# First two batches' memory matrix loaded dense on SP's queue and padded by POOL, first loads reordered: attention with memory and a gated MLP on one Trainium2 core

## The chip, the cores and the metric

The kernel runs on one core of a Trainium2 chip. The metric is the device time of one execution in microseconds (us); a kernel's time is the median over its runs. Engines are named as in the profile: PE (TensorE), DVE (VectorE), ACT (ScalarE), POOL (GpSimd) and SP (SyncE, which here only issues DMAs).

## The reference

Causal attention, mixed with a retrieval from a memory matrix M, followed by RMS norm and a gated MLP. B, H, S, D = 4, 8, 576, 64; the MLP has 2304 tokens, width 512 and inner width 1536, and its three weights arrive as float64.

```python
def _attn_ref(q, k, v, M_prev, z_prev, beta):
    scores = scale * np.matmul(q, k.transpose(0, 1, 3, 2))
    scores = np.where(causal, -1000000000.0, scores)
    a = np.exp(scores - scores.max(-1, keepdims=True))
    a /= a.sum(-1, keepdims=True) + 1e-09
    local = np.matmul(a, v)
    q_p = np.where(q > 0, q, np.exp(q) - 1.0) + 1.0
    mem_ret = np.einsum('bhsd,bhde->bhse', q_p, M_prev)
    mem_norm = np.einsum('bhsd,bhd->bhs', q_p, z_prev)[..., None] + 1e-06
    g = 1.0 / (1.0 + np.exp(-beta))[None, :, None, None]
    return g * mem_ret / mem_norm + (1 - g) * local
def _moe_ref(x, w_gate, w_val, w_out, rms_g):
    xn = x / np.sqrt(np.mean(x * x, axis=-1, keepdims=True) + 1e-06) * rms_g
    g = xn @ w_gate
    return (g / (1.0 + np.exp(-g)) * (xn @ w_val)) @ w_out
```

## The kernel before, in words

The 2304 tokens are 18 blocks of 128 rows; a block holds all 8 heads, 512 numbers of k, of v and of q per row. Blocks 0 and 1 are the first rows of batches 0 and 1. They are computed in float32, ahead of all else, so that the first chunk (two blocks) of the MLP can begin early. Later blocks use pairs of float16 numbers and transposes by DMA.

**The head, blocks 0 and 1** (L1026 to L1037). For a block n, PE transposes k and q (`prep_qk32`, L363), ACT and DVE make phi(q) (`phi_calc`, L347 to L349), PE makes the scores (`scores32`, L416), DVE masks them and finds the row minimum (L421), ACT takes the exponential (L430). PE transposes phi(q) and multiplies it with M (`mem32`, L442). M's place for this, `Mz`, is padded: 65 numbers per head in a row, of which the first 64 are M's and number 64 is z, so that one matmul gives both mem_ret and mem_norm. Its two halves of 64 partitions are equal copies of M, because heads with even and odd number lie in different halves; of the eight matmuls of a block, four read one half and four the other. Then `pv32` (transposes of the exponentials and L453), `evac32` (L465 to L482), `x_norm` and `x_float` (L696, L699) give the block's x, and xT0 of both blocks is what the first projections read (`m_proj`, L850).

**The weights.** w_gate and w_val come as 24 pieces of 128 x 512 float64 (512 KB each; w0 to w7 are the first third, t = 0, and so on) into a ring of six places. Each piece is converted by one ACT cast (L766) and two DVE operations (L767, L768). When a piece is converted, its place is free and the piece six later is loaded (`load_w`, L736). w_out's 12 pieces follow in the same way (`load_wo`, L756).

**The first loads.** `setup_small` puts beta, rms_g and z (twice) on ACT's queue. `HORD` (L26) gives the order of the first big loads: q0, k0, M0, q1, k1, M1, w0 to w5, where "k" brings k and v of a block. q, k, v and w go on SP's queue. M of the batches 0 and 1 goes on ACT's queue (L218), straight into the padded place; M of the batches 2 and 3 comes later, on SP's queue. POOL puts z into the padding (L222). POOL also issues eight loads of 256 KB (`load_pre`, L746), of k and v of later blocks of batches 0 and 1, for the column sums that set the scales (`gram`, L145); six are issued at once, two when places are free.

**What sets the order.** An engine takes its instructions in program order, and a scheduler writes that order from priorities and its own estimate of times; it decides anew for a changed program, also far behind the change. The loads of SP's and ACT's queues take eight completion semaphores in turn, both queues from one set; a load that is given a semaphore in use waits, on the engine that issues it, until the load that had it before has landed. Loads on POOL's queue have a set of their own.

Of the kernel before, what the change touches and what calls it, by code (L numbers as in the profile page):

```python
# [9 lines left out]
F32 = mybir.dt.float32  # L10
F16 = mybir.dt.float16
# [11 lines left out]
XSCALE = 2.0 ** 11  # L23
NEG = -1.0e38
HP = 0
HORD = "q0 k0 M0 q1 k1 M1 w0 w1 w2 w3 w4 w5"  # L26
LAG = 3
LAG0 = 8
NA = 2
# [27 lines left out]
def attn_memory_moe_kernel(  # L57
# [12 lines left out]
    nc = tc.nc  # L70
    B, D, H = M_prev.shape[:3]
# [3 lines left out]
    P = 128  # L75
# [11 lines left out]
    sb = ctx.enter_context(tc.tile_pool(name="sb", bufs=2))  # L87
# [50 lines left out]
    def gram(acc, src, first, last):  # L138
# [12 lines left out]
        out=ident, in_=ident, compare_op=ALU.is_equal, fill=0.0,  # L151
# [47 lines left out]
    def load_kv(n):  # L199
        tag = "kvt" if is_tail[n] else "kv"  # L200
        stage[n] = sb.tile([P, 2, HD], F32, tag=tag, name=f"kv{n}", bufs=1 if is_tail[n] else 4)
        if n < 2:
            for j in range(2):
                nc.sync.dma_start(out=stage[n][:, j], in_=qkv[n, :, j, :])
        else:
            nc.sync.dma_start(out=stage[n], in_=qkv[n, :, :2, :])

    def load_M(b):
        if b < 2:
            t = sb.tile([P, H, VW], F16, tag="v16", name=f"Mz{b}", bufs=10)  # L210
            Mz[b] = t.bitcast(F32)
            qst[("M", b)] = Mz[b][:, :, :D]
        else:
            qst[("M", b)] = sb.tile([P, HD], F32, tag="q", name=f"M{b}").rearrange(
                "p (h e) -> p h e", h=H
            )
        for hf in range(2):
            (nc.scalar if b < 2 else nc.sync).dma_start(  # L218
                out=qst[("M", b)][hf * D : (hf + 1) * D], in_=M_prev[b]
            )  # L220
        if b < 2:
            nc.gpsimd.tensor_copy(Mz[b][:, :, D], zz[:, b * H : (b + 1) * H])  # L222

    def load_q(n):
# [3 lines left out]
    def square_acc(src, acc):  # L228
        junk = sb.tile([P, HD], BF16, tag="junk", name="junk", bufs=1)
        np_ = src.shape[0]  # L230
        if len(src.shape) == 3:
            dst = junk[:np_].rearrange("p (h e) -> p h e", e=src.shape[2])
        else:
            dst = junk[:np_, : src.shape[1]]
        nc.scalar.activation(dst, src, AF.Square, accum_out=acc)  # L235
# [31 lines left out]
    def stat_M(b):  # L267

        cb[b] = const.tile([P, 8 + 2 * H], F32, name=f"cb{b}")
        ssm = tiny.tile([P, 3], F32, tag="mx", name=f"ssm{b}", bufs=2)  # L270
        square_acc(qst[("M", b)], ssm[:, 0:1])
        pow2_scales(over_partitions(ssm[:, 0:1], 1), 1, cb[b][:, 2:3], cb[b][:, 5:6])
        prep_M(b)

# [22 lines left out]
            tcb[b // 2] = t  # L297

    def prep_M(b):
        src = qst.pop(("M", b))  # L300
        m = sb.tile([P, 2, H, D + 2], F16, tag="M16", name=f"M16_{b}")
        M16[b] = m
        hi_cast(m[:, 0, :, :D], src, cb[b][:, 2:3])
        lo_cast(m[:, 1, :, :D], src, cb[b][:, 2:3], m[:, 0, :, :D])
        nc.gpsimd.tensor_copy(m[:, :, :, D], zhl[:, :, b * H : (b + 1) * H])
# [611 lines left out]


    def setup_small():
        nc.scalar.dma_start(out=beta_sb, in_=beta.rearrange("(o h) -> o h", o=1).to_broadcast([P, H]))  # L920
        nc.scalar.dma_start(out=rg, in_=rms_g)
        for r in range(2):
            nc.scalar.dma_start(out=zz[r * D : (r + 1) * D], in_=z_prev)

    gmax2 = const.tile([P, 1], F32, name="gmax2")

# [93 lines left out]
    pcs = [(m, cc, t) for t in range(NT3) for m in range(2) for cc in range(NC)]  # L1020
    setup_small()
    with tc.high_priority(HP) if HP else contextlib.nullcontext():
        for x in HORD.split():
            {"q": load_q, "k": load_kv, "M": load_M, "w": lambda p: load_w(*pcs[p])}[x[0]](int(x[1]))
    setup_consts()
    with tc.high_priority(PRIO[0]):  # L1026
        for n in range(2):
# [247 lines left out]
```

## Time and profile before

| what | value |
|---|---|
| timed runs | 654.41, 654.85, 657.68 us; median 654.85 us |
| the profiled execution | 659.15 us, of which the recorded span is 657.5 us |
| PE busy | 598.7 us (91% of the span) |
| DVE busy | 469.1 us (71%) |
| ACT busy | 384.5 us (58%) |
| POOL busy | 168.3 us (26%) |
| DMA, mean over the span | 135 GB/s |
| granted TensorE clock, mean over the span | 0.977 of full speed |

How to read it: the profile is one execution, and its times are counted from the start of the span. Busy time is that of instructions; a wait is put down to what ended it. The shares are averages over a span with very different stretches, so a question about the head is answered by views of the head: the lists of waits for a window, the timeline, and the table by stretches, which gives for each stretch the busy time and number of instructions of every engine, the granted clock (PEclk, 1.00 is 2.4 GHz and 0.50 is 1.2 GHz), the mean busy share of the 16 DMA engines and the GB/s that they moved.

### The profile page before, as it was taken

To read this page: it belongs to the slowest core of one execution; us is meant where nothing else is said; L and a number is where in the kernel's file an instruction comes from. 1 tells how busy PE (TensorE), PEld (TensorE's weight loads), DVE (VectorE), ACT (ScalarE), POOL (GpSimd) and SP (SyncE) were. 2 spreads that over 40 slices of the span, in tenths; PEclk is the share of its full clock that TensorE was granted. 3 is DMA by queue.
4 is the path that set the end of the run, shared out by engine and by line. 5 is a ranking of instruction groups with operands and counts; after the bars stand their busy time and mean duration, and the time that the engine had idled before them with its cause. 6 is when DMAs were issued, how large, how long until landed. Compare 5 with 4: busy or idle time off the path is not lost.

```text
span 657.5 us, 15991 instructions
## 1 busy us (share of the span) xinstructions
PE 598.7 (91%) x6120; PEld 467.7 (71%) x6120; DVE 469.1 (71%) x1444; ACT 384.5 (58%) x803; POOL 168.3 (26%) x251
## 2 busy tenths in 40 slices
PE   4569988997989679998999999899999999999996
PEld 3457876646757467786878677778777778878774
DVE  5489998878998656796876857968777667872221
ACT  4355667577688757575666656856666544442322
POOL 3020131122382323231242311522332212212211
PEclk9598998999999989999999999999999999999999
DMA  8897699639248798346848773495676573440001
GB/s 265 299 336 285 170 307 234 109 60 234 57 84 162 161 174 160 75 87 128 166 101 162 145 122 73 83 175 104 123 122 117 87 97 86 78 82 17 33 1 33
DMA packets 190636, 88.63 MB, mean 135 GB/s; under 512 B 175968, under 2 KB 175968, under 8 KB 190560
## 3 DMA queue, kind: packets, MB, share of 16 engines
q1 hardware_dynamic: 187360, 84.96, 60.3%
q0 software_dynamic: 640, 2.10, 0.9%
q8 instruction: 48, 0.79, 0.5%
q10 hardware_dynamic: 2560, 0.55, 0.5%
q14 instruction: 28, 0.23, 0.1%
HBM read 36.20 MB, written 4.72 MB: 62 GB/s over the span
## 4 chain that ended last, share of the span: by engine, by line
PE 50%; DMA 18%; DVE 17%; ACT 8%; issue 4%; SPq 1%; POOL 1%; ACTq 0%; DVEq 0%
PE gv L857 24%; DMA PT<-P 6%; PE out L912 4%; PE out L913 4%; PE out L914 4%; DMA kv<-in_qkv_dram 3%; DMA Mz<-in_M_prev_dram 2%; PE sc L500 2%; DVE P L566 2%; DMA xT<-x 2%; PE sc L526 2%; ACT junk L235 2%; DVE S L506 2%; DMA wo<-in_moe_w_out_dram 2%; DMA kT<-row 1%
## 5 line engine op out<-in xcount | busy, mean ns | idle before, releaser
L857 PE MATMUL gv<-xT,wgv 128*128 128x256 f16 x2304 | 314.1, 274 | 4.9 <-DVE th L871 2.9
L857 PEld LDWEIGHTS <-wgv 128*128 128x128 f16 x2304 | 220.9, 98 | 40.8 <-issue 6.7
L883 POOL TENSOR_TENSOR h<-th,h 128x256 f16<-128x256 f32 x96 | 72.0, 750 | 266.8 <-ACT h L882 214.4
L552 ACT ACTIVATE S<-S,nm 128x256 f32<-128x256 f32 (+4 forms) x128 | 75.4, 611 | 50.5 <-DVE nm L513 36.4
L500 PE MATMUL sc<-kT,qT 128*128 128x128 f16 x608 | 84.6, 220 | 2.0 <-DVE nm L506 1.4
L566 DVE TENSOR_TENSOR P<-S,P 128x512 f16<-128x512 f32 (+2 forms) x84 | 63.1, 751 | 31.5 <-ACT P L557 31.1
L868 DVE SCALAR_TENSOR_TENSOR th<-th,gv 128x256 f32<-128x256 f32 x96 | 39.8, 415 | 60.6 <-ACT th L867 60.2
L867 ACT ACTIVATE th<-gv,wt 128x256 f32<-128x256 f32 x96 | 45.0, 468 | 49.9 <-PE gv L857 49.7
L913 PE MATMUL out<-wo,h 128*128 128x512 f16 x192 | 73.1, 381 | 0.0
L912 PE MATMUL out<-wo,h 128*128 128x512 f16 x192 | 72.6, 382 | 0.2 <-ACT h L882 0.2
L914 PE MATMUL out<-wo,h 128*128 128x512 f16 x192 | 71.9, 380 | 0.0
L506 DVE CUSTOM_DVE_ANT_0 S<-sc,mask,qsc 128x256 f32<-128x256 f32 (+3 forms) x112 | 62.0, 574 | 10.0 <-PE sc L500 7.9
L557 ACT CAST P<-S 128x512 f16<-128x512 f32 (+2 forms) x100 | 59.7, 597 | 13.9 <-DMA PT<-P 12.4
L882 ACT CAST h<-th 128x256 f16<-128x256 f32 x96 | 38.6, 402 | 45.1 <-DVE th L871 44.5
L590 PE MATMUL loc<-v,PT 128*128 128x65 f16 x304 | 49.8, 194 | 16.3 <-DMA PT<-P 15.7
L500 PEld LDWEIGHTS <-qT 128*128 128x128 f16 x608 | 50.6, 98 | 7.2 <-issue 1.6
L592 PE MATMUL loc<-v,PT 128*128 128x65 f16 x304 | 49.5, 194 | 0.0
L591 PE MATMUL loc<-v,PT 128*128 128x64 f16 x304 | 49.5, 194 | 0.0
L850 PE MATMUL gv<-xT,wgv 128*128 128x256 f32 x192 | 46.1, 392 | 2.2 <-DVE h32e L871 1.8
L871 DVE SCALAR_TENSOR_TENSOR th<-th,wt,gv 128x256 f32<-128x256 f32 x96 | 45.7, 477 | 1.7
L590 PEld LDWEIGHTS <-PT 128*128 128x128 f16 x304 | 29.3, 98 | 23.1 <-DMA PT<-P 19.2
L850 PEld LDWEIGHTS gv<-xT,wgv 128*128 128x128 f32 x192 | 36.2, 195 | 8.1 <-DVE h32e L871 2.0
(222 smaller groups left out, 1096.6 us busy)
## 6 DMA issues: line engine op xcount, KB each, us to landing
kv<-in_qkv_dram SPq DMA_DIRECT2D x16, 512.0 KB, 4.8
wo<-in_moe_w_gate_dram SPq DMA_DIRECT2D x12, 512.0 KB, 7.4
wo<-in_moe_w_val_dram SPq DMA_DIRECT2D x12, 512.0 KB, 4.9
q<-in_qkv_dram SPq DMA_DIRECT2D x18, 256.0 KB, 3.5
wo<-in_moe_w_out_dram SPq DMA_DIRECT2D x8, 512.0 KB, 5.3
qT<-qT SPq DMA_DIRECT2D x32, 128.0 KB, 2.5
out_dram<-res SPq DMA_DIRECT2D x16, 256.0 KB, 2.3
pre<-in_qkv_dram POOLq DMA_DIRECT2D x8, 256.0 KB, 8.5
```

Of the source, the lines that this page charges most:

```text
L500: nc.tensor.matmul(t[:, g * w + j * P : g * w + (j + 1) * P], qT[n][:, t2, h, :], kT[blk_of[(b, j)]][:, h, :], start=(t2 == 0), stop=(t2 = ...
L506: nc.vector.tensor_tensor_reduce(out=s[:, g * w : (g + 1) * w], in0=t[:, g * w : (g + 1) * w], in1=mask[:, m0 : m0 + w], scale=qsc[n][:, 5:6],
L552: nc.scalar.activation(v_, v_, AF.Exp, bias=nm[:, g : g + 1], scale=-1.0)
L557: nc.scalar.copy(p16[:, : G * w], s[:, : G * w])
L566: eng.tensor_tensor(p16[:, w : 2 * w], s[:, :w], p16[:, :w], ALU.subtract)
L590: nc.tensor.matmul(a, phi_, vhi, start=(j == 0), stop=False)
L850: nc.tensor.matmul(o, wgv[:, 1 + p, o0 : o0 + P], xT[0][:, cc, :], start=(cc == 0), stop=(cc == NC - 1))
L857: nc.tensor.matmul(o, lhs, xT[c][:, rhs, :], start=(cnt == 0), stop=(cnt == 3 * NC - 1))
L883: nc.gpsimd.tensor_tensor(h16[:, 1], th, h16[:, 0], ALU.subtract)
L912: nc.tensor.matmul(o, hh, whi, start=(f == 0), stop=False)
L913: nc.tensor.matmul(o, hh, wlo, start=False, stop=False)
L914: nc.tensor.matmul(o, hl, whi, start=False, stop=(f == NF - 1))
```

## The change

M of the batches 0 and 1 is loaded on SP's queue into a dense tile (128 x 512, from the slots of `row16`, which the later blocks' splits use), and POOL copies it into the padded place; ACT's sum of squares of M reads the dense tile. k and v of the blocks 0 and 1 become loads of their own, and `HORD` is now k0, q0, M0, k1, q1, v0, M1, v1, w0 to w5. z, beta and rms_g are loaded on POOL's queue, z first.

```diff
-HORD = "q0 k0 M0 q1 k1 M1 w0 w1 w2 w3 w4 w5"
+HORD = "k0 q0 M0 k1 q1 v0 M1 v1 w0 w1 w2 w3 w4 w5"
...
-        if n < 2:
-            for j in range(2):
-                nc.sync.dma_start(out=stage[n][:, j], in_=qkv[n, :, j, :])
-        else:
+        if n >= 2:
             nc.sync.dma_start(out=stage[n], in_=qkv[n, :, :2, :])
+
+    def load_half(n, j):
+        nc.sync.dma_start(out=stage[n][:, j], in_=qkv[n, :, j, :])
...
             t = sb.tile([P, H, VW], F16, tag="v16", name=f"Mz{b}", bufs=10)
             Mz[b] = t.bitcast(F32)
-            qst[("M", b)] = Mz[b][:, :, :D]
+            t = sb.tile([P, H, 2, D], F16, tag="row16", name=f"M{b}")
+            qst[("M", b)] = t.rearrange("p h t e -> p (h t e)").bitcast(F32).rearrange(
+                "p (h e) -> p h e", h=H
+            )
...
         for hf in range(2):
-            (nc.scalar if b < 2 else nc.sync).dma_start(
-                out=qst[("M", b)][hf * D : (hf + 1) * D], in_=M_prev[b]
-            )
+            nc.sync.dma_start(out=qst[("M", b)][hf * D : (hf + 1) * D], in_=M_prev[b])
         if b < 2:
+            nc.gpsimd.tensor_copy(Mz[b][:, :, :D], qst[("M", b)])
             nc.gpsimd.tensor_copy(Mz[b][:, :, D], zz[:, b * H : (b + 1) * H])
...
-        square_acc(qst[("M", b)], ssm[:, 0:1])
+        square_acc(qst.pop(("M", b)), ssm[:, 0:1])
...
-        src = qst.pop(("M", b))
+        src = Mz[b][:, :, :D] if b < 2 else qst.pop(("M", b))
...
-        nc.scalar.dma_start(out=beta_sb, in_=beta.rearrange("(o h) -> o h", o=1).to_broadcast([P, H]))
-        nc.scalar.dma_start(out=rg, in_=rms_g)
         for r in range(2):
-            nc.scalar.dma_start(out=zz[r * D : (r + 1) * D], in_=z_prev)
+            nc.gpsimd.dma_start(out=zz[r * D : (r + 1) * D], in_=z_prev)
+        nc.gpsimd.dma_start(out=beta_sb, in_=beta.rearrange("(o h) -> o h", o=1).to_broadcast([P, H]))
+        nc.gpsimd.dma_start(out=rg, in_=rms_g)
...
+        load_kv(0), load_kv(1)
+        way = {
+            "q": load_q, "k": lambda n: load_half(n, 0), "v": lambda n: load_half(n, 1),
+            "M": load_M, "w": lambda p: load_w(*pcs[p]),
+        }
         for x in HORD.split():
-            {"q": load_q, "k": load_kv, "M": load_M, "w": lambda p: load_w(*pcs[p])}[x[0]](int(x[1]))
+            way[x[0]](int(x[1]))
```

From the change on, line numbers are 2 or 3 higher up to L919 or so (L442 becomes L444, L766 becomes L768) and more behind it.

What stands where, as the built programs have it. First, SP's queue at the start, before (a row of kv0 or kv1 with x2 is the load of k and that of v; wo is the ring of six weight places):

```order
L226 DMA q0_96<-in_qkv_dram 128x512
L204 DMA kv0_98<-in_qkv_dram 128x512 x2
L226 DMA q1_105<-in_qkv_dram 128x512
L204 DMA kv1_107<-in_qkv_dram 128x512 x2
L736 DMA wo_84<-in_moe_w_gate_dram 128x512 x4
L736 DMA wo_84<-in_moe_w_val_dram 128x512 x2
```

and of the change:

```order
L206 DMA kv0_96<-in_qkv_dram 128x512
L228 DMA q0_99<-in_qkv_dram 128x512
L221 DMA M0_102<-in_M_prev_dram 64x512 x2
L206 DMA kv1_97<-in_qkv_dram 128x512
L228 DMA q1_108<-in_qkv_dram 128x512
L206 DMA kv0_96<-in_qkv_dram 128x512
L221 DMA M1_112<-in_M_prev_dram 64x512 x2
L206 DMA kv1_97<-in_qkv_dram 128x512
L738 DMA wo_84<-in_moe_w_gate_dram 128x512 x4
L738 DMA wo_84<-in_moe_w_val_dram 128x512 x2
```

The four loads of M came over from ACT's queue and stand, with all of k, q and v, ahead of w0 (before, q0, k0, v0, q1, k1 and v1 did).

Second, DVE's row up to block 1's scores (`S_209` and `S_213` with `nm32`), before; the third and the fourth L768 of the program are the two in it:

```order
L469 SCALAR_TENSOR_TENSOR den_164<-mem0_1_180,gsig_85 128x4
L472 RECIPROCAL den_164<-den_164 128x16
L476 TENSOR_TENSOR t1_0_280<-mem0_0_179,den_164 128x4x64
L476 TENSOR_TENSOR t1_0_280<-mem0_1_180,den_164 128x4x64
L767 TENSOR_SCALAR wo_84<-wo_84 128x512
L367 COPY q32_1_196<-tp_237 128x512
L768 SCALAR_TENSOR_TENSOR wgv_83<-wgv_83,wo_84 128x512
L767 TENSOR_SCALAR wo_84<-wo_84 128x512
L768 SCALAR_TENSOR_TENSOR wgv_83<-wgv_83,wo_84 128x512
L421 ISA S_209,nm32_211<-sc_207,mask_72 128x128
```

and of the change, where the three L770 in it are the fourth to the sixth:

```order
L471 SCALAR_TENSOR_TENSOR den_168<-mem0_1_184,gsig_85 128x4
L770 SCALAR_TENSOR_TENSOR wgv_83<-wgv_83,wo_84 128x512
L769 TENSOR_SCALAR wo_84<-wo_84 128x512
L474 RECIPROCAL den_168<-den_168 128x16
L369 COPY q32_1_200<-tp_241 128x512
L770 SCALAR_TENSOR_TENSOR wgv_83<-wgv_83,wo_84 128x512
L478 TENSOR_TENSOR t1_0_284<-mem0_0_183,den_168 128x4x64
L478 TENSOR_TENSOR t1_0_284<-mem0_1_184,den_168 128x4x64
L769 TENSOR_SCALAR wo_84<-wo_84 128x512
L770 SCALAR_TENSOR_TENSOR wgv_83<-wgv_83,wo_84 128x512
L423 ISA S_213,nm32_215<-sc_211,mask_72 128x128
```

Block 1's scores stand behind the conversion of w5 now, and stood behind that of w3.

Third, SP's queue at the first transposes of the later blocks (kT0 and qT2; the rows ahead are pieces of w_out), before:

```order
L736 DMA wo_84<-in_moe_w_val_dram 128x512 x4
L756 DMA wo_84<-in_moe_w_out_dram 128x512 x4
L319 DMA_TRANSPOSE kT0_572<-row16_569 128x8x128
L319 DMA_TRANSPOSE qT2_602<-row16_599 128x8x128
L206 DMA kv4_586<-in_qkv_dram 128x1024
```

and of the change:

```order
L738 DMA wo_84<-in_moe_w_val_dram 128x512 x4
L758 DMA wo_84<-in_moe_w_out_dram 128x512 x6
L321 DMA_TRANSPOSE kT0_576<-row16_573 128x8x128
L321 DMA_TRANSPOSE qT2_606<-row16_603 128x8x128
L203 DMA kv4_590<-in_qkv_dram 128x1024
```

Two loads of w_out moved ahead of the first transposes.

## Rows read from the trace of the kernel before

**Rows 1.** The page's first part: busy time, share of the span, instructions.

```profile
PE 598.7 (91%) x6120; PEld 467.7 (71%) x6120; DVE 469.1 (71%) x1444; ACT 384.5 (58%) x803; POOL 168.3 (26%) x251
```

**Rows 2.** PE's waits in 0 to 60 us: total us, times, longest us.

```profile
PE mem L442 <- DMA Mz<-in_M_prev_dram: 10.1, 1, 10.1
```

**Rows 3.** SP's waits in 0 to 130 us: total us, times, longest us.

```profile
SPq L736 <- DMA Mz<-in_M_prev_dram: 14.4, 2, 11.3
...
SPq L756 <- DVE wo L767: 6.1, 1, 6.1
```

**Rows 4.** Timeline, 0 to 25 us: start, us, engine, line, operation, count [idle before].

```profile
5.46 0.63 ACTq L218 DMA_DIRECT2D Mz<-in_M_prev_dram  x1
...
6.31 5.41 SPq L736 DMA_DIRECT2D wo<-in_moe_w_gate_dram  x4
...
7.76 1.67 ACTq L218 DMA_DIRECT2D Mz<-in_M_prev_dram  x2
...
8.82 3.53 POOL L746 DMA_DIRECT2D pre<-in_qkv_dram  x6 [0.25 <-issue]
...
11.76 12.22 SPq L736 DMA_DIRECT2D wo<-in_moe_w_val_dram  x2
...
23.68 1.97 PE L442 MATMUL mem<-Mz,q 64*128 64x65 f32 x8 [10.12 <-DMA Mz<-in_M_prev_dram]
```

**Rows 5.** Table by stretches: busy us (count) per engine, PEclk, DMA share, GB/s.

```profile
0.00:5.00 5.00, 0.00 (x0) 0.00 (x0) 0.81 (x5) 1.38 (x2) 0.93 (x8) 1.00 0.42 106
5.00:10.00 5.00, 3.60 (x18) 2.93 (x20) 2.25 (x4) 1.57 (x3) 1.56 (x6) 1.00 1.03 306
10.00:15.00 5.00, 3.56 (x26) 2.87 (x24) 4.86 (x27) 3.08 (x14) 2.60 (x9) 1.00 1.03 352
15.00:20.00 5.00, 0.00 (x0) 0.00 (x0) 1.32 (x5) 1.66 (x7) 0.00 (x0) 0.60 1.04 374
20.00:25.00 5.00, 1.32 (x6) 1.32 (x7) 0.00 (x0) 0.00 (x0) 0.00 (x0) 0.50 0.69 138
25.00:30.00 5.00, 5.00 (x32) 4.27 (x31) 3.82 (x10) 2.27 (x4) 0.00 (x0) 0.54 0.94 343
30.00:35.00 5.00, 3.36 (x34) 2.70 (x32) 4.83 (x27) 4.23 (x18) 0.00 (x0) 1.00 1.02 405
...
55.00:60.00 5.00, 5.00 (x24) 3.72 (x22) 4.34 (x19) 2.44 (x6) 1.09 (x3) 1.00 0.95 337
```

**Rows 6.** DMA issues: count, KB each, median us from issue to landing.

```profile
pre<-in_qkv_dram POOLq DMA_DIRECT2D x8, 256.0 KB, 8.5
...
Mz<-in_M_prev_dram ACTq DMA_DIRECT2D x4, 128.0 KB, 15.1
...
zz<-in_z_prev_dram ACTq DMA_DIRECT2D x2, 8.0 KB, 3.9
```

**Rows 7.** Timeline, 23 to 60 us, block 1 on DVE, first projections on PE.

```profile
29.93 0.28 DVE L421 CUSTOM_DVE_ANT_0 S<-sc,mask 128x128 f32<-128x128 f32 x1
...
52.62 0.69 DVE L699 TENSOR_TENSOR xT<-xtp,rg 128x512 f32<-128x512 f32 x1 [0.15 <-PE xtp L696]
...
55.15 3.72 PE L850 MATMUL gv<-xT,wgv 128*128 128x256 f32 x16
```

**Rows 8.** Timeline, 76 to 84 us, POOL and DVE side by side.

```profile
77.02 2.67 POOL L115 TENSOR_TENSOR v<-kv,v 128x512 f16<-128x512 f32 x2 [7.56 <-ACT v L112]
...
77.13 1.56 DVE L96 SCALAR_TENSOR_TENSOR row<-q,qsc,row 128x512 f16<-128x512 f32 x1
...
78.62 1.62 DVE L768 SCALAR_TENSOR_TENSOR wo<-wo 128x512 int32<-128x512 int32 x1
```

**Rows 9.** Conversion of weights, by line: ns shortest, median, longest; first and last start.

```profile
L766 ACT ACTIVATE wgv<-wo x24: 640/662/702, 12.3 to 68.5; 128x512 f32<-128x512 f32 x24
...
L768 DVE SCALAR_TENSOR_TENSOR wgv<-wgv,wo x24: 668/689/699, 14.4 to 69.6; 128x512 int32<-128x512 int32 x24
...
L767 DVE TENSOR_SCALAR wo<-wo x32: 405/422/1297, 12.5 to 98.7; 128x512 int32<-128x512 int32 x32
```

## Prediction

> **What bounds the kernel now.** I read the page first. PE is busy for 91% of the span [rows 1], so over most of the run only PE's own work counts, and a change to loads can gain only where PE stands idle. The list of PE's waits, for the first 60 us alone, names one such place: the matmuls of L442 (q features times M) waited 10.1 us, once, for the DMA that brings M [rows 2]. The timeline shows the place: ScalarE issues the first half of M0 at 5.46, the second from 7.76, and block 0's L442 matmuls that read the second half start at 23.68 [rows 4]; all of block 1's work on PE stands behind them. M takes 15.1 us from issue to landing (median) for 128 KB [rows 6].
>
> M delays more than PE. The list of SP's own waits gives 14.4 us in two waits at L736 for M's DMA [rows 3]. These are loads of weight pieces (w0 to w23, in the order of loading): w3 and w5 each reuse a completion semaphore that a half of M0 still holds. So SP, which issued w4 at 11.76, was through with w5 only 12.22 us later [rows 4], and q2, kv2 and all the next loads stood behind it.
>
> Why is M slow? The table by stretches is the view for that. From 5 to 20 us the 16 DMA engines are busy at 1.03 to 1.04 of their time and move 306 to 374 GB/s; then, from 20 to 25, with SP stuck, 138 GB/s [rows 5]. So M shares saturated engines with weights that are not wanted yet, and nobody fills the gap behind it. VectorE does 1.32 us of work in 15 to 20 and none in 20 to 25 [rows 5].
>
> **The change, part by part.** Each load is 256 KB for a half of k, v or q, 128 KB for a half of M, 512 KB for a weight piece.
>
> *M on SP's queue, ahead of the weights.* In the new order M0, q1, v0, M1 and v1 all stand before w0: six halves of k, q, v and four halves of M, 2048 KB or 2.10 MB. The old kernel had moved 5 x 0.106 + 5 x 0.306 = 2.06 MB by 10.0 us [rows 5], so all of this is in by about 10.1 and M1, which is not last, by about 9.5: long before the 23.68 of now. The 10.1 us wait goes, and so does SP's wait.
>
> *What is late next.* In the new row of VectorE the conversions of all six first weight pieces stand before block 1's scores; before, four did. So block 1 now waits for w5. Behind the 2.10 MB come w0 to w5 (3.15 MB), and POOL's six early loads (1.57 MB) share the engines: 4.72 MB at the mean of the two full stretches, (352 + 374) / 2 = 363 GB/s [rows 5], is 13.0 us, so w5 lands at 23.1. Its cast on ScalarE (0.66) and merge on VectorE (0.69) [rows 9] bring the scores to 24.5, where now they start at 29.93 [rows 7]. **Gain: 5.4 us**, not 10. Bounds: at the lowest saturated rate, 306 [rows 5], the 4.72 MB take 15.4 us and the gain is 3.0. At the highest in these rows, 405, and with w5 ahead of all of POOL's loads, 3.15 MB take 7.8 us, the scores could start at 19.2, and then the old wait of 10.1 caps the gain. I take the middle rate because it comes from the stretches with the same mix of queues.
>
> *From there to the projections.* Block 1's scores at 29.93 and the end of its x, 52.62 + 0.69 = 53.3 [rows 7], are 23.4 us apart, nearly all of it VectorE work in both kernels; 24.5 + 23.4 = 47.9. Does a load hold that up? In the new row the last x step (0.69) stands right behind the first operation on w14 (0.42 [rows 9]; before, it was w13). With w14 have come fifteen weight pieces, a w_out piece, kv2, kv3, kv8, q2, q3, the 2.10 MB and POOL's eight loads, 14.7 MB: 10.1 + 12.6 / 0.363 = 44.8, and 1.1 more is 45.9, below 47.9. So the 5.4 us live on, and the projections, which keep PE at 5.00 of 5.00 from 55 to 60 [rows 5], start 5.4 us sooner than 55.15 [rows 7]. Behind them each step waits for PE, VectorE or a transfer that these release, so all of it moves along.
>
> *POOL's two copies of M* (128x512). No row has a one-input copy of this size. Below, nothing; above, the two-input subtraction of the same shape, 2.67 for two or 1.34 each [rows 8]. I take the upper end: 2.7 us of POOL. M0 lands at 0.53 MB + 0.306 per us, for 1.05 MB, at 6.7, and its copy ends by 8.1, while the matmuls that need it stand behind block 0's scores. M1's copy ends by 10.9, and block 1 waits for weights until after 23. Cost nothing; without that cover, 1.34. Behind it on POOL wait the two memsets and the six early loads. They were issued from 8.82 on [rows 4] and start some 2 us later; they land 8.5 us after issue [rows 6], the last near 23, and feed the column sums that PE reaches only after block 1's scores. Nothing.
>
> *The copies beside VectorE.* At 77 us POOL's L115 ran beside VectorE, and there L96 took 1.56 and a merge (L768) 1.62 [rows 8], where a merge takes 0.69 [rows 9]. So a copy can cost VectorE up to 0.93 at a time, 1.9 for both. I take nothing, since VectorE idles before w5; uncovered, it is C below. The Trainium skill (SBUF — State Buffer, section "SBUF: two separate sides") states that the two engines hold a common port pair as an exclusive lock for a whole instruction, so that one fully blocks. The rows agree in kind, with 0.93 of the other's 1.34; by the rule alone the two copies would take 2.7 us from VectorE, and the sum, uncovered, would be 652.2.
>
> *Tiny loads on POOL's queue.* Four issues at 3.53 / 6 = 0.59 [rows 4] put 2.4 us before POOL's mask, which is wanted only with block 0's scores. z is issued first, by some 2.3 us, lands 3.9 us later [rows 6], at 6.2, and is wanted at M0's 6.7. *k0 ahead of q0* brings PE's first transposes forward by one issue, under 0.5 us. Both end in the wait for w5: nothing.
>
> **The sum.** -5.4 on the profiled 659.15 us is 653.75. The median of the timed runs is 654.85, 0.65% below the profiled execution, so the forecast is 654.85 - 5.4 = **649.5 us**.
>
> **The rivals.** A measurement here can tell about 0.5%, 3.3 us, from no change.
>
> A. *The whole wait goes.* If w4 and w5 come as soon as SP is free, block 1 is not held and the 10.1 us go entire: 644.8. For it: SP no longer stalls. Against: the engines are full from 5 to 20. 0.13.
>
> B. *The transfers bind through w14.* At 306 GB/s the 12.6 MB take 41.2 us: w14 at 51.3, the last x at 52.4 against 53.3 before. Then the gain is 0.9: 653.9. For it: 306 is a measured rate of saturated engines. Against: from 10 on the rows say 343 or more wherever SP is not stuck. 0.19.
>
> C. *The copies block VectorE* in its chain: 1.9 of the 5.4 is given back, 651.4. Against: the chain idles right behind. 0.08.
>
> D. *Slower: SP's first transposes queue behind two more weight loads.* SP is in order, and six w_out loads now stand before the transposes of kT0 and qT2 where four did. Such a load waited 6.1 us for VectorE, once [rows 3]. Two such waits would hold the transposes 12.2 us, and block 2's scores with them; less the 5.4, that is 6.8 slower: 661.7. It decides against the change by more than 0.5% once the two wait over 8.7 us together. Against: a slot is freed at VectorE's pace, and VectorE too is 5.4 us earlier. 0.10.
>
> My forecast has the remaining 0.50. Faster by over 0.5%: my case, A, and half of C, 0.67; B and the other half of C are the same, 0.23; slower is D, 0.10. The range goes from A's 644.8 to 655, which takes in B, my bounds (10.1 and 3.0) and leaves D out.
>
> **What would show it.** Right: no wait of L444 for M in PE's list; M landing under 8 us; block 1's scores on VectorE between 23 and 26.5, waiting for a weight piece; the 20 to 25 stretch above 300 GB/s; the first projections near 49.8, and the last instruction as much earlier. A would show scores before 21; B, x steps that wait for w12 to w14; C, VectorE operations over 1.3 us beside the two copies before 11 us; D, SP waiting over 8.7 us at the two w_out loads. I am wrong if the projections start sooner and the end does not move, which would say that a later stage takes the gain back.

## The result, and the profile after

| | before | after |
|---|---|---|
| median | 656.26 us | 666.54 us |
| timed runs | 654.41, 654.85, 657.68, 661.63 | 664.68, 665.55, 667.54, 670.95 |
| the profiled execution | 659.15 us, span 657.5 | 670.95 us, span 669.3 |

The changed kernel takes 1.014 [1.009, 1.019] times as long (95% interval in brackets, here and below): it is slower, by some 10 us. (Before was run once more beside it, so its median is not the one shown ahead.) What the change aimed at happened nearly as forecast, and the time was lost behind it.

**The head.** PE's waits of after in 0 to 60 us (total, times, longest), the longest three:

```profile
PE tp L365 <- DMA kv<-in_qkv_dram: 3.6, 1, 3.6
PE sc L418 <- ACT q L367: 3.4, 1, 3.4
PE xtp L698 <- DVE diag L692: 2.9, 1, 2.9
```

The wait of 10.1 us for M [rows 2] is gone. The four loads of M of the batches 0 and 1 land after a median of 5.8 us, where they took 15.1 in [rows 6]. The view of the tile M in 0 to 30 us has:

```profile
DMA to landing us min/median/max: 3.7/5.8/6.3
```

After's timeline, in order of time, with the points that answer to [rows 4] and [rows 7]:

```profile
6.34 2.95 SPq L738 DMA_DIRECT2D wo<-in_moe_w_gate_dram  x4
...
7.78 0.61 POOL L223 COPY Mz<-M 128x512 f32<-128x512 f32 x1 [3.36 <-DMA M<-in_M_prev_dram]
...
8.03 0.39 DVE L939 TENSOR_SCALAR gsig<-gsig 128x8 f32<-128x8 f32 x1 [0.98 <-ACT gsig L938]
...
10.32 0.84 SPq L738 DMA_DIRECT2D wo<-in_moe_w_val_dram  x2
...
10.97 1.97 PE L444 MATMUL mem<-Mz,q 64*128 64x65 f32 x16
...
11.42 0.61 POOL L223 COPY Mz<-M 128x512 f32<-128x512 f32 x1 [2.75 <-DMA M<-in_M_prev_dram]
...
23.92 0.28 DVE L423 CUSTOM_DVE_ANT_0 S<-sc,mask 128x128 f32<-128x128 f32 x1
...
46.79 0.69 DVE L701 TENSOR_TENSOR xT<-xtp,rg 128x512 f32<-128x512 f32 x1 [0.72 <-PE xtp L698]
...
50.50 0.80 PE L852 MATMUL gv<-xT,wgv 128*128 128x256 f32 x1
```

SP has issued w5 at about 11.2 instead of 24. Block 1's scores start at 23.92 (29.93 before), the last x at 46.79 (52.62), the first projection at 50.50 (55.15). The stretch from 20 to 25 us (busy us and count of PE, PEld, DVE, ACT, POOL; PEclk, DMA share, GB/s) stands against that of [rows 5]:

```profile
20.00:25.00 5.00, 3.67 (x24) 3.35 (x24) 4.51 (x19) 2.60 (x7) 0.00 (x0) 1.00 1.03 406
```

From 20 to 25 us the engines move 406 GB/s where 138 stood, and VectorE is busy for 4.51 us where it did nothing. At the first projection, at 50.50 us, the change is 4.65 us ahead.

One column needs care, here and in the first rows of [rows 5]: the PEclk of 1.00. In the trace the clock has no record ahead of its first change (at 12.5 us in before, 33.3 in after, 29.9 in e1, which is explained below), and the view counts a stretch without a record as full speed. Block 1's 16 matmuls with M, in before at a recorded 1.00 and in after inside the stretch without a record, say otherwise:

```profile
30.11 1.11 PE L442 MATMUL mem<-Mz,q 64*128 64x65 f32 x16
```

```profile
25.24 1.98 PE L444 MATMUL mem<-Mz,q 64*128 64x65 f32 x16
```

The float32 matmuls of 128 x 128 tell the same: in the stretch without a record most start 214 ns apart in both kernels, and at a recorded 1.00 most start 109 to 116 ns apart. So after runs its head at the lower level, 1.2 GHz, up to about 33 us, and before up to 12.5 and again from 16.0 to 29.6. The mean clocks of the pages leave the first of these stretches out.

**Behind the head.** The lead is lost and a lag grows. The table has the time (us) at which some points of the program are reached; a chunk's projections are twelve groups, and e1 and e5 are explained below. Each column is one execution: four kernels with the same loads and the same order up to the first projection (e1, e5, e7, e8) reach it at 48.44 to 50.05, so a difference of less than some 2 us says little.

| point | before | after | e1 | e5 |
|---|---|---|---|---|
| chunk 0, first projection | 55.15 | 50.50 | 48.48 | 48.44 |
| chunk 0, fourth group | 68.66 | 65.94 | 61.98 | 61.74 |
| block 2's first scores (L502) | 81.90 | 81.80 | 75.22 | 76.71 |
| chunk 0, twelfth group | 112.61 | 116.33 | 104.61 | 111.69 |
| chunk 1, first projection | 147.07 | 154.01 | 138.73 | 149.86 |
| chunk 2, first projection | 230.91 | 243.23 | 221.80 | 236.67 |
| chunk 3, first projection | 298.31 | 312.37 | 288.87 | 307.39 |
| chunk 6, first projection | 480.23 | 491.78 | 467.58 | 487.25 |

After is 4.65 us ahead at chunk 0, level at block 2, 6.94 late at chunk 1 and 12.32 late at chunk 2; 14.06 at chunk 3 and 11.55 at chunk 6, which stays so to the end. This is where the two programs differ: comparing the order in which each engine takes its instructions, 1,169 of PE's 5,920 matmuls behind the first loads stand elsewhere, the last of them at PE's 1,507th, and 528 of VectorE's 1,268 operations, the last at its 556th, which before runs at 233 us. Behind that point the orders are identical. Nothing in the diff asks for it: the scheduler decided the order anew.

The page's first part and clock line of after:

```profile
PE 612.4 (92%) x6120; PEld 477.4 (71%) x6120; DVE 473.7 (71%) x1444; ACT 385.0 (58%) x803; POOL 171.3 (26%) x257
...
PEclk9988998798999969999899999999999999999999
```

Against [rows 1] PE does the same 6,120 matmuls in 13.7 us more; its idle time (span less busy) is 56.9 against 58.8. So in these two profiles the loss does not show as more waiting, but as matmuls at a lower granted clock. Counting the stretch without a record as half speed, PE is busy at half speed for 58.0 us in after and 26.6 in before; take half of that off the busy time, and 583.4 and 585.4 us are left, nearly the same. Of the 58.0 us, 22.2 lie in that first stretch (6.1 in before). They are not what makes the change slow: e1, the fastest kernel below, has 22.0 there. The other 35.8 (20.5 in before) follow in part from waits, as the experiments show.

### The profile page after: what moved, and what is told of

The parts are those of the page before. It is cut to its first block, busy times and chain, and to the rows that moved or that the text cites. A ratio compares the mean times of both kernels' runs of the same rounds, so it can differ in the third digit from the quotient of the medians.

```text
span 669.3 us, 15998 instructions
## 1 busy us (share of the span) xinstructions
PE 612.4 (92%) x6120; PEld 477.4 (71%) x6120; DVE 473.7 (71%) x1444; ACT 385.0 (58%) x803; POOL 171.3 (26%) x257
## 4 chain that ended last, share of the span: by engine, by line
PE 67%; DMA 14%; DVE 7%; issue 4%; ACT 3%; SPq 1%; POOL 1%; ACTq 0%; POOLq 0%; DVEq 0%
PE gv L859 33%; DMA PT<-P 6%; PE out L915 6%; PE out L916 6%; PE out L914 6%; PE sc L502 4%; PE sc L528 2%; PE out L906 2%; DMA pre<-in_qkv_dram 2%; DMA kv<-in_qkv_dram 2%; PE gv L852 2%; DMA wo<-in_moe_w_out_dram 1%; DMA kT<-row 1%; PE loc L592 1%; PE mem L629 1%
## 5 line engine op out<-in xcount | busy, mean ns | idle before, releaser
L502 PE MATMUL sc<-kT,qT 128*128 128x128 f16 x608 | 83.8, 220 | 5.3 <-DMA qT<-qT 2.0
L870 DVE SCALAR_TENSOR_TENSOR th<-th,gv 128x256 f32<-128x256 f32 x96 | 39.8, 416 | 57.3 <-ACT th L869 56.9
L592 PE MATMUL loc<-v,PT 128*128 128x65 f16 x304 | 50.5, 195 | 14.5 <-DMA PT<-P 14.3
L502 PEld LDWEIGHTS <-qT 128*128 128x128 f16 x608 | 50.7, 98 | 12.1 <-DMA qT<-qT 2.4
L852 PE MATMUL gv<-xT,wgv 128*128 128x256 f32 x192 | 48.7, 407 | 3.5 <-DVE h32v L873 2.2
L594 PE MATMUL loc<-v,PT 128*128 128x65 f16 x304 | 50.2, 195 | 0.0
L852 PEld LDWEIGHTS gv<-xT,wgv 128*128 128x128 f32 x192 | 37.5, 202 | 10.1 <-DVE h32v L873 2.4
```

What stands on the lines that cost most here:

```text
L502: nc.tensor.matmul(t[:, g * w + j * P : g * w + (j + 1) * P], qT[n][:, t2, h, :], kT[blk_of[(b, j)]][:, h, :], start=(t2 == 0), stop=(t2 = ...
L592: nc.tensor.matmul(a, phi_, vhi, start=(j == 0), stop=False)
L852: nc.tensor.matmul(o, wgv[:, 1 + p, o0 : o0 + P], xT[0][:, cc, :], start=(cc == 0), stop=(cc == NC - 1))
```

## The experiments

The theory: the loads gain what was forecast, and the new *order* behind them costs more. Its rival: something in the *loads* themselves (the copies, SP's queue, the tiny loads) costs it. To tell them apart I built kernels in which a written table sets the order of every engine behind the first loads, whatever the scheduler would choose. It adds links between neighbours that fix only who is issued first; the kernel before with its own order written down in this way builds to the same program, instruction for instruction, as without. Below, `before` and `after` are the orders of the two kernels, taken from the built programs. `cut(x, y, p)` is x's order up to the point p of the program, and behind it the remaining instructions in y's. `place(x, y, s)` is x's order with the instructions s put at the places that they have in y's. Ratios are to the kernel before, which ran again beside every group (medians 657.4 to 658.5 us).

### Group A: the order or the loads

**e1**: after's loads and copies, before's order behind them.

```diff
+def in_order(tc):
...
+    for engine, steps in table.items():
+        row = [i for i in block if str(i.engine) == "EngineType." + engine]
+        at, last = 0, None
+        for k, step in enumerate(steps):
+            at += step
+            if last is not None:
+                tc.add_manual_dep(
+                    row[at], last.name,
+                    mybir.DependencyInfo(mybir.DependencyClass.NoSync, mybir.DependencyReason.DATA), reason="order",
+                )
+            last = row[at]
...
         attn_memory_moe_kernel(tc, *args)
+        in_order(tc)
```

> The kernel after, with every engine's instructions behind the first loads chained in the order in which they stand in the kernel before. Theory O (the scheduler's remade order, which differs on PE up to its 1,507th matmul, costs what the head gains, and more): the head's gain lives on, the ratio to before is 0.984 to 0.994, some 4 to 10 us under before. Theory L (the moved loads themselves cost later, by their traffic or by the buffers that M holds): the order changes nothing, ratio 1.010 to 1.019 as after. Theory C (the projections start earlier but at a lower granted clock): the lead of 4.66 us at the first projections is still mostly lost by 60 us, ratio 0.995 to 1.000.

Measured: 0.982 [0.980, 0.985], median 648.12 us.

**e2**: the converse, before's loads with after's order.

```diff
-order = before
+order = after
```

> The kernel before, its loads untouched, with every engine's instructions behind the first loads chained in the order in which they stand in the kernel after. Theory O: the order's cost without the head's gain, ratio 1.014 to 1.030 (9 to 20 us over before). Theory L: no change, 0.997 to 1.003.

Measured: 1.015 [1.011, 1.019], 670.13 us.

**e3** and **e4**: the scheduler is left free, and two loads trade places, in before and in after. By the built programs this alone moves 1,003 and 785 matmuls.

```diff
-HORD = "q0 k0 M0 q1 k1 M1 w0 w1 w2 w3 w4 w5"
+HORD = "q0 k0 M0 q1 k1 M1 w0 w1 w2 w3 w5 w4"
```

```diff
-HORD = "k0 q0 M0 k1 q1 v0 M1 v1 w0 w1 w2 w3 w4 w5"
+HORD = "k0 q0 M0 k1 q1 v0 M1 v1 w0 w1 w2 w3 w5 w4"
```

> The kernel before with the loads of the last two of its six first weight pieces, w4 and w5, traded; the scheduler is free, and moves 1,003 of 5,920 matmuls to another place. Theory O: the time moves by more than the trade of two loads can explain, by 3 us or more to either side (ratio outside 0.995 to 1.005); within that, the order is not as sensitive as the theory needs, or this order happens to be as good. Theory L: within 2 us of before, as the same bytes come in the same queue.

> The kernel after with the loads of w4 and w5 traded; the scheduler is free and moves 785 of 5,920 matmuls. Theory O: the time moves away from that of after by 3 us or more to either side, with the first projections still near 50.5 us. Theory L: within 2 us of after, ratio 1.011 to 1.017 to before.

Measured: e3 1.000 [0.997, 1.003], 658.67 us; e4 1.005 [1.002, 1.008], 661.73 us.

What follows: with before's order the new loads gain 1.8%; with after's order nothing that can be told (1.014 against 1.015). After's order costs 1.5% with the old loads and 1.4 + 1.8 = 3.2% with the new. So the order costs the time and not the loads. e4 agrees: the same change, with two loads traded and another order decided for it, is 0.9% better, though its first projection comes 2.2 us later (52.69). e3 does not: 1,003 matmuls moved and the time stayed, where the theory expected a move of 0.5% or more. So another order can cost time, and need not. e1 beats both kernels, and gains more than the 5.4 us that were forecast: 1.8% are some 11 us. Its page:

```profile
PE 600.2 (93%) x6120; PEld 469.7 (73%) x6120; DVE 469.2 (73%) x1444; ACT 383.0 (59%) x803; POOL 172.5 (27%) x257
...
PEclk9989998999999799999999999999999999999999
```

Against after, whose matmuls are the same, it has 12.2 us less busy time on PE and 12.0 less idle time (645.1 − 600.2 = 44.9): between these two profiles the order's cost is half waits, half clock (PE is busy at half speed for 32.7 us in e1, 25.3 less than in after). The lead holds in e1 all the way, as its column of the table shows: 6.67 us at the first projection, 6.68 at block 2, 8.00 at the twelfth group and 12.65 at chunk 6. Why it grows there was not settled.

### Group B: where in the order

Here both parts of the program have after's loads, and the order changes hands at a point: the first projection (F0), block 2's scores (sc2), or the first projection of chunk 1 (c1).

```diff
-order = before
+order = cut(before, after, F0)
```

> The loads of after; every engine in before's order up to PE's first projection matmul, in after's order from there. The traces of e1 and after part by 2.0 us at that matmul, by 5 at block 2's scores, by some 13 at chunk 1's first projection and by 21 to 24 from 260 us on. Theory S (each stage of after's order costs its own share): only the head's share of 2 to 5 us comes back, ratio to before 1.002 to 1.012. Rival H (the head's order sets all that follows): nearly all comes back, 0.982 to 0.990.

```diff
-order = before
+order = cut(after, before, F0)
```

> The loads of after; after's order up to PE's first projection matmul, before's from there. Theory S: e1's time plus the head's share of 2 to 5 us, ratio 0.985 to 0.992. Rival H: as after, 1.010 to 1.019.

```diff
-order = before
+order = cut(before, after, sc2)
```

> The loads of after; before's order up to PE's first scores of block 2 (L502), after's from there. Theory S: the 5 us up to there come back, the 16 to 19 behind stay, ratio 1.003 to 1.010. Rival E (what stands before block 2's scores, SP's and VectorE's w_out loads and conversions among it, sets the rest): 0.982 to 0.990.

```diff
-order = before
+order = cut(after, before, sc2)
```

> The loads of after; after's order up to PE's first scores of block 2, before's from there. If only what stands behind those scores loses (as e7 says), the head's share of some 5 us is all that is lost against e1: ratio 0.986 to 0.994. Rival: what stands before them (six w_out loads ahead of SP's first transposes) sets the rest, 1.000 or more.

```diff
-order = before
+order = cut(before, after, c1)
```

> The loads of after; before's order up to PE's first projection matmul of chunk 1 (L859), after's from there. Theory S: what is lost behind chunk 1's first projection, some 8 us, stays: ratio 0.992 to 0.998. Rival E or H: 0.982 to 0.990.

| run | ratio | median us |
|---|---|---|
| e5 | 1.011 [1.006, 1.016] | 665.71 |
| e6 | 0.988 [0.984, 0.992] | 649.74 |
| e7 | 1.014 [1.008, 1.019] | 667.74 |
| e11 | 0.992 [0.989, 0.996] | 653.38 |
| e8 | 0.996 [0.993, 1.000] | 654.74 |

What follows: no single place has it. Of the 3.2%, after's order costs 0.6 up to the first projection (e6 less e1), 0.4 more up to block 2's scores (e11 less e6) and 1.4 behind chunk 1's first projection (e8 less e1); if the parts added, the remaining 0.8 would lie between block 2 and chunk 1. Each of these is good to about 0.5, so the 0.4 is not told from nothing. And the parts do not simply add: between block 2 and chunk 1, e7 less e8 gives 1.7, and e7 and e11 together give 3.1 + 1.0 = 4.1. e7 lies above both ranges that were expected of it. One reason is in PE's waits of e7 behind the seam, a wait that neither whole order has:

```profile
PE csum L145 <- DVE wmx L789: 6.2, 1, 6.2
```

**How an order costs time twice.** PE's waits from 75 to 130 us, of after and then of e1:

```profile
PE allp L132 <- DVE nm L508: 2.4, 2, 1.9
PE gv L852 <- DVE h32v L873: 2.2, 1, 2.2
PE loc L592 <- DMA PT<-P: 2.1, 2, 1.3
PE sc L502 <- DMA qT<-row: 1.8, 1, 1.8
PE sc L502 <- DMA qT<-qT: 1.3, 1, 1.3
PE gv L852 <- DVE h32e L873: 1.3, 1, 1.3
```

```profile
PE loc L592 <- DMA PT<-P: 2.7, 1, 2.7
PE gv L852 <- DVE h32e L873: 1.5, 1, 1.5
PE allp L132 <- DVE nm L508: 0.4, 1, 0.4
```

All are short, and the totals of these rows are 11.1 and 4.6 us. But two of the eight in after, of 2.2 and 1.9 us, are followed by a slower clock, and in e1 the longest. After's table in steps of 2 us, around its two (columns as in [rows 5]):

```profile
106.00:108.00 2.00, 0.47 (x2) 0.45 (x3) 2.00 (x6) 2.00 (x6) 0.00 (x0) 1.00 0.81 159
108.00:110.00 2.00, 2.00 (x8) 1.59 (x7) 2.00 (x7) 0.30 (x2) 0.00 (x0) 0.60 0.98 174
110.00:112.00 2.00, 2.00 (x7) 1.61 (x6) 1.71 (x9) 0.91 (x2) 0.00 (x0) 0.54 1.11 255
...
124.00:126.00 2.00, 0.47 (x3) 0.23 (x4) 2.00 (x12) 0.00 (x0) 0.00 (x0) 0.87 0.68 131
126.00:128.00 2.00, 2.00 (x32) 1.58 (x30) 1.90 (x9) 1.05 (x3) 0.72 (x1) 0.50 0.04 8
128.00:130.00 2.00, 2.00 (x21) 1.89 (x19) 1.34 (x10) 2.00 (x6) 0.75 (x2) 0.50 0.00 0
130.00:132.00 2.00, 2.00 (x10) 1.42 (x8) 1.17 (x10) 0.92 (x2) 0.73 (x1) 0.50 0.01 4
```

PE stands idle for about 1.5 us of a row, with VectorE busy for all of it, and the rows behind it run at half speed, 1.2 GHz, or near it: two rows in which some 1.7 us of work are lost, and in the second place three with 3.0 lost. That is about as much again as the wait took, or more. The Trainium skill (TensorE: Matmul & The Clock Gate, section "HAM oscillation — how this bites in real kernels") says that gaps between matmuls bring the clock down and that the work behind each gap starts slow; these two waits agree, the six others do not show it. The lower clock is also seen at the seam of the head. After's and then e1's stretches around the first projections:

```profile
45.00:50.00 5.00, 5.00 (x34) 4.23 (x34) 3.52 (x10) 3.59 (x8) 0.11 (x1) 0.50 0.92 308
50.00:55.00 5.00, 5.00 (x16) 3.81 (x16) 4.20 (x18) 0.87 (x2) 0.69 (x3) 0.62 0.94 312
```

```profile
45.00:50.00 5.00, 5.00 (x40) 4.33 (x40) 4.70 (x16) 3.08 (x6) 0.52 (x1) 0.80 0.90 328
50.00:55.00 5.00, 5.00 (x25) 3.71 (x24) 4.36 (x20) 3.56 (x9) 0.58 (x2) 1.00 0.96 343
```

PE is busy for all ten microseconds in both, and after gets 50 matmuls done where e1, at nearly the same place of the program, does 65 (not all of one size).

### Group C: which steps

A candidate from the order itself: six loads of w_out ahead of SP's first transposes where before has four. SP's timeline of e5 and then of e1, which have the same loads and the same order up to the projections:

```profile
59.42 9.94 SPq L758 DMA_DIRECT2D wo<-in_moe_w_out_dram  x6
70.50 1.35 SPq L321 DMA_TRANSPOSE kT<-row  x1
...
103.42 3.56 SPq L570 DMA_TRANSPOSE PT<-P  x2
```

```profile
62.05 5.39 SPq L758 DMA_DIRECT2D wo<-in_moe_w_out_dram  x4
68.51 1.35 SPq L321 DMA_TRANSPOSE kT<-row  x1
...
96.99 1.25 SPq L570 DMA_TRANSPOSE PT<-P  x1
```

The first transpose is 2.0 us later in e5, the first of P (L570) 6.4. So I moved the 96 instructions of w_out (12 loads, 12 casts, 24 VectorE steps, 48 column sums) from one order to the other and left the rest: in e9 from after's order to before's places, in e10 the reverse, both with after's loads; then, behind the projections alone, w_out's steps only (e13) and all steps but those (e14).

```diff
-order = after
+order = place(after, before, w_out)
```

> The loads and the order of after, except that the 96 instructions of w_out (12 loads on SP, 12 casts on ScalarE, 24 steps of the conversion on VectorE, 48 column sums on PE) stand on each engine at the places that they have in before's order. Theory W (in the order of after the w_out work stands too early, and the steps of blocks 2 and 3 queue behind its transfers): most of the loss comes back, ratio to before 0.985 to 0.997. Rival A (the steps of blocks 2 and 3 themselves, and the projections, stand in a worse order): nothing comes back, 1.008 to 1.019.

```diff
-order = before
+order = place(before, after, w_out)
```

> The reverse: the loads of after in the order of before, the 96 instructions of w_out at the places that they have in after's order. Theory W: most of the loss appears, 0.997 to 1.015. Rival A: as e1, 0.980 to 0.988.

```diff
-order = before
+order = place(before, cut(before, after, F0), w_out)
```

> e1 (after's loads, before's order) with the 96 instructions of w_out alone at the places that they have in e5 (after's order from the first projection on), so that none is moved ahead of the projections as in e10. e5 is 1.011 and e1 0.982 of before. Theory W (w_out's steps too early make the loss): 0.998 to 1.012. Rival A (the other steps do): 0.980 to 0.988. If both share it: between, and e14 as much below 1.011 as this is above 0.982.

```diff
-order = before
+order = place(cut(before, after, F0), before, w_out)
```

> The reverse: e5's order with the 96 instructions of w_out at the places that they have in before's order. Theory W: 0.980 to 0.990. Rival A: 1.003 to 1.012.

| run | ratio | median us |
|---|---|---|
| e9 | 1.011 [1.005, 1.017] | 664.80 |
| e10 | 1.006 [1.002, 1.010] | 662.31 |
| e13 | 0.998 [0.995, 1.001] | 655.04 |
| e14 | 1.011 [1.007, 1.016] | 664.98 |

What follows: w_out's places are not the cause by themselves. Put back, they recover a third of a per cent (e9 against after's 1.014), which the intervals do not tell from nothing. All other steps of after's order, with w_out's left alone, cost as much as the whole (e14 equals e5). w_out's steps alone cost something too, 1.5% (e13 less e1), so the two do not add either, and the mixed orders again have waits of their own. In PE's waits of e13 there is one that makes up half of the 7.0 us between the two profiled spans, 652.1 us and e1's 645.1:

```profile
PE csum L145 <- DVE wmx L789: 3.5, 1, 3.5
```

e10 is not clean evidence: taking after's places, its w_out pieces also come early, and VectorE waits for one in front of block 1 (VectorE's waits of e10):

```profile
DVE rawo L769 <- DMA rawo<-in_moe_w_out_dram: 3.6, 1, 3.6
```

Its lead over before, 7.5 us at block 1's scores, is gone at 40 us. Which single step of after's order costs the most was not found, and after these runs I doubt that there is one: hundreds of steps stand otherwise, and each of the other mixtures of the two orders costs something too, from 0.6% (e6) up. That is an argument and not a proof.

### Group D: what of the loads gains

Here the order is before's throughout, except in e15, and parts of the change are made alone or undone.

**e12**: the kernel before, with only M of batches 0 and 1 on SP's queue, still straight into the padded place.

```diff
-            (nc.scalar if b < 2 else nc.sync).dma_start(
+            nc.sync.dma_start(
```

> The kernel before with one edit, M's four loads issued by SP in place of ScalarE, still into the padded tile and with no copy, in before's order. Theory P (M's place ahead of the weights is what gains): as e1, ratio 0.980 to 0.988. Rival N (the padded rows of 256 B are what makes M slow, so that the dense landing and POOL's copy are needed): M still lands late and the ratio is 0.992 to 1.003.

**e16**: e1, with M straight into the padded place on SP's queue and no copy.

```diff
-            qst[("M", b)] = t.rearrange("p h t e -> p (h t e)").bitcast(F32).rearrange(
-                "p (h e) -> p h e", h=H
-            )
+            qst[("M", b)] = Mz[b][:, :, :D]
...
-            nc.gpsimd.tensor_copy(Mz[b][:, :, :D], qst[("M", b)])
```

> e1 (after's loads in before's order) without the dense landing: SP loads M straight into its padded place and POOL copies nothing. e12 (the kernel before with M on SP, padded, alone) is 0.988 of before, e1 0.982. If the dense landing is what parts them: as e12, 0.984 to 0.992. If it is the order of the first loads: as e1, 0.979 to 0.985.

**e17**: e1, with beta, rms_g and z on ACT's queue as before.

```diff
-            nc.gpsimd.dma_start(out=zz[r * D : (r + 1) * D], in_=z_prev)
+            nc.scalar.dma_start(out=zz[r * D : (r + 1) * D], in_=z_prev)
```

> e1 with the four tiny loads back on ScalarE's queue. The prediction counted them as nothing: as e1, 0.979 to 0.986. If they matter (ScalarE's first operations come later behind their issues), 0.986 to 0.992.

**e15**: after's loads with e3's order, a third order that the scheduler chose by itself.

```diff
-order = before
+order = e3
```

> The loads of after in the order of e3 (the kernel before with two loads traded, whose own time was 1.0001 of before). If an order's worth goes with the order, this is as fast as e1, 0.980 to 0.988. If before's order is fast with these loads by chance, 0.995 or more.

| run | ratio | median us |
|---|---|---|
| e12 | 0.988 [0.983, 0.992] | 651.57 |
| e16 | 0.996 [0.993, 0.998] | 654.94 |
| e17 | 0.992 [0.988, 0.995] | 651.49 |
| e15 | 0.995 [0.992, 0.998] | 655.26 |

What follows. M's place on SP's queue, ahead of the weights, is worth 1.2% alone (e12). In the new order of loads the dense landing with its copy is worth 1.3% (e16 less e1; e16 lies above both ranges that were expected of it). But M does not land sooner for it. The four loads of M in the first 30 us, of e1 (dense) and of e16 (padded):

```profile
DMA to landing us min/median/max: 3.7/6.1/6.8
```

```profile
DMA to landing us min/median/max: 3.9/6.2/6.8
```

What differs is POOL. In e1 its copies wait for M, and its six early loads stand behind them; in e16 they stand behind z's small copies alone. POOL's timelines of e1 and of e16:

```profile
12.52 3.21 POOL L748 DMA_DIRECT2D pre<-in_qkv_dram  x6
```

```profile
6.08 3.21 POOL L744 DMA_DIRECT2D pre<-in_qkv_dram  x6
```

In e16 these 1.57 MB come among the first weights: w0 lands at 16.65 us instead of 13.53, and PE has one long wait in the head, so that the first projection is 4.7 us later than in e1:

```profile
PE tp L361 <- DVE k L365: 5.3, 1, 5.3
```

So what the rows say for the copies is that they hold POOL's loads back. No run held those loads back alone, so this is argued and not shown.

The tiny loads on POOL's queue, to which I gave nothing, are worth 0.9% (e17 less e1), but not by the head, which is 0.33 us later in e17. The page of e17:

```profile
PE 605.5 (93%) x6120; PEld 473.4 (73%) x6120; DVE 469.0 (72%) x1444; ACT 383.2 (59%) x803; POOL 171.0 (26%) x253
```

Its idle time, 649.6 − 605.5 = 44.1, is close to e1's 44.9; its matmuls take 5.3 us longer at a mean clock of 0.981 against 0.989. The difference lies behind the head: the granted clock is 0.95, 0.83 and 0.96 from 130 to 160, 200 to 240 and 280 to 320 us, and 1.00, 0.91 and 1.00 in e1. Why was not settled. And e15 shows that the gain belongs to a pair: the same loads gain 1.8% with before's order, 0.5% with e3's (0.995 against e3's own 1.000), next to nothing with after's.

## Why the prediction was wrong

The head came as its steps have it. M's second halves landed at 7.64 and 11.37 (forecast 6.7 and 9.5), late but under the cover that was named; w5 landed at 22.56 (23.1), block 1's scores started at 23.92 (24.5) and the first projection at 50.50 (49.8). "What is late next" was right: w5, and so a gain at the scores of 6.0 us (5.4) and not 10. Two workings were off without harm. The 1.05 MB for M0 is too much, as k0, q0 and M0 are 0.79 MB, which would give 5.8 us. And against B it was said that the rows show 343 GB/s or more from 10 us on wherever SP is not stuck, but the whole table of before has 310 in 40 to 45 us and 216 in 45 to 50.

The copies were over-priced. They took 0.61 us each, not 1.34, and hid. One VectorE operation met the first of them: it took 0.39 us, where the operation on the same data takes 0.17 in before, and ended at 8.42, right behind the copy's end at 8.39. By the lock rule of the Trainium skill (SBUF — State Buffer, section "SBUF: two separate sides") it had to wait for the copy's end; the rows agree. It cost 0.2 us in a stretch with idle time, so nothing, and C did not happen. The delay of POOL's six loads was put at 2 us and at nothing; they were issued from 12.04 instead of 8.82, and e16 says that this delay may be a part of the gain.

**The step that failed** is "Behind them each step waits for PE, VectorE or a transfer that these release, so all of it moves along." It holds if the steps behind stay in their order: e1 has the same loads and copies and before's order, and there the lead of 6.7 us at the first projection is still 6.7 at block 2 and more later. (So 5.4 us was too small as well: with the order held, the change gains some 11.) But the scheduler had put 1,169 matmuls and 528 VectorE operations elsewhere, up to 240 us. I looked at the new order at three places, counted the moved instructions of the head, and took the rest for the same. In after that order turned a lead of 4.65 us at the first projection into a lag of 12.3 at chunk 2. The prediction's last test, that the projections start sooner and the end does not follow, is what happened, and "a later stage takes the gain back" is the place; the mechanism is the order, which was no rival in it.

Rival D was on the right side for a part of the reason, though its sign did not show. SP's longest wait at L758, 7.5 us, stands in front of the first of the six w_out loads (before has such a wait of 6.1 there [rows 3]). The fifth and the sixth, which are the two of D, waited some 4 us together and not 8.7. What they cost can be bounded by e9, which has w_out's steps back at before's places and so four loads ahead of the transposes. SP's timelines of after and of e9:

```profile
63.44 9.83 SPq L758 DMA_DIRECT2D wo<-in_moe_w_out_dram  x6
74.65 1.36 SPq L321 DMA_TRANSPOSE kT<-row  x1
```

```profile
60.98 8.56 SPq L758 DMA_DIRECT2D wo<-in_moe_w_out_dram  x4
70.55 1.35 SPq L321 DMA_TRANSPOSE kT<-row  x1
```

In after the first transpose of kT comes at 74.65 against 75.28 in before, and block 2's scores at 81.80 against 81.90; in e9 at 70.55 and 77.39. So D, with the other moved steps of w_out, ate most of the head's lead. It is no more than that. With after's order kept up to block 2's scores and before's behind them (e11) the kernel is still faster than before, so D's price of 6.8 us slower is not reached there; and e9, with D undone, is nearly as slow as after. What makes the change slow lies mostly behind it. A (no scores before 21), B (no x step waits for w12 to w14) and C did not happen.

A smaller miss is the tiny loads, at nothing: 0.9%, with a cause that is open.

## What to carry to other kernels

Where a scheduler writes the order, an edit of the first 25 us is also a new draw of the order far behind it, and that draw can cost more (here 1.5 to 3.2%) than the edit gains (1.8%), or nothing (e3). So compare the whole order of both programs before forecasting, to the last instruction that differs, and when judging an edit hold the order of the rest fixed, in both kernels. The version to keep here is e1: the change, with the old order written down behind it, 648.12 us.

## What the runs showed of the hardware

- Two PE waits of 2.2 and 1.9 us among dense matmuls were followed by 4 and 6 us at a granted clock of 0.50 to 0.60 (after, 106 to 112 and 124 to 132 us); six others of 0.5 to 1.8 us in 75 to 130 us were not. e1 has it too, behind its wait of 2.7 us (a row of e1's table in steps of 2 us): fewer waits, not none, make it the faster one.

```profile
105.00:107.00 2.00, 2.00 (x7) 1.56 (x6) 1.86 (x7) 1.22 (x4) 0.00 (x0) 0.50 0.77 270
```

- A PEclk of 1.00 ahead of the first recorded change of the clock is not a measurement: there the same 16 matmuls took 1.98 us (after) that took 1.11 at a recorded 1.00 (before).
- Loads of 128 KB that land in pieces of 64 numbers (256 bytes) into a padded place took as long as dense ones at the same places of the queue: 3.9 to 6.8 us (e16) and 3.7 to 6.8 (e1).
- GpSimd's one-input copy of 128 x 512 float32 took 0.61 us, about half of the two-input subtraction of that shape with a float16 result (L115 in before: median of eight 1.12, and 1.34 each for the two of [rows 8]).
- Two kernels with nearly the same idle time on PE (e1 and e17, one execution each) differ by 5.3 us in the time that the same matmuls take. What decides on the clock there is open.
